# Attention in plain float32 on four 64x64 quarters of the array

## The chip, the cores and the metric

The kernel runs on one core of a Trainium2 chip. The time is the device time of one execution in microseconds. Before the change it is 1518.6 us, the median of three runs (1517.89 to 1519.48). A core has engines that run beside each other, each with its own list of instructions in order: PE (TensorE, matrix products; its weight loads are shown as PEld), DVE (VectorE), ACT (ScalarE), POOL (GpSimd) and SP, whose list issues most DMAs.

## What is computed

The reference, cut to what matters (q, k and v are 8 x 8 x 576 x 64; x has 4608 tokens of 512):

```
chunk = 64                                    # each head attends within chunks of 64 tokens
scores = (q_c @ k_c.T) / sqrt(64)
attn = exp(scores - max(scores)); attn = attn / (sum(attn) + 1e-9)
x = attn @ v_c                                # then heads side by side: 4608 x 512
h = x @ w_in;  g = softplus(h);  x = g @ w_out                # 512 -> 2048 -> 512
out = max(x @ w1, x @ w2, x @ w3) @ w_out2                    # 512 -> 768 -> 512
```

The inputs of the two layers (weights) are float64 in their stored form, so the kernel converts them first.

## The kernel before

**Tiles.** The 4608 tokens are cut into 9 blocks of 512 (TB), the 8 heads into 4 pairs (HP). A tile `t` of attention is one block and one pair of heads; there are 36, of which the first 8 (`attention_first`) come while weights are still converted and the other 28 (`attention`) while the first layer runs. A tile holds 8 chunks for each of two heads, 16 small problems of 64 x 64.

**Two ways of multiplying.** The large products (`mlp1`, lines 748 and 768) cut each float32 operand into a rounded high part and the rest, a low part, and add three fast products (high x high, high x low, low x high: `PASS`). The later tiles do so too: `do_s` (L672) makes the scores of a tile from 4 x 3 matmuls, `do_v` (L725) the second products (softmax times v) from 8 x 3. As a matmul contracts over 128 partitions and a problem has 64, one operand is laid out as blocks with zeros beside them (`fill`, into slots that POOL sets to zero in `zeros`, L1101). The first eight tiles use plain float32 matmuls, with zeros too (`big["f", t]`, set by DVE at L508): turns of q and k through a product with the identity (`turn_in`, L531), scores (L562), a turn of the softmax (`turn`, L522) and second products (L611). The later tiles turn q and k with DVE's transpose of 32 x 32 blocks (L638, L643) and the softmax with such a transpose (L700) and a trip through DRAM (`pd`, L704 and L708).

**From scores to x.** The softmax (L484 to L489) works on an SBUF copy of the scores; `to_x` copies the second products from PSUM as high part and subtracts for the low part, in two halves, since the result of `do_v` stands on 64 partitions.

**What sets the order.** All work is a list of operations with costs per engine, due times and buffers. A planner (`Plan.order`) goes through it in simulated time: when an engine is idle it takes the ready operation with the earliest due time whose buffers are free. What comes out is the fixed order of every engine. PSUM has the buffers `ph` (two of one bank), `acc` (two of two banks, the sums of a block) and `aps` (one of two banks), which the later tiles use for scores and products. Tile `t` has its scores due two steps and its products 0 steps ahead of `due_v`; a step is one slice of 128 hidden columns of the first layer. DMAs of q, k, v and of the trip through DRAM are issued from SP's list.

Names: `s` are general slots in SBUF (weights, x, operands), `tmp` smaller ones, `g` the softplus output, `mx` the maxima and sums. L254, L256 and L261 are the lines of the helpers `copy_op` (ACT, DVE) and `tt_op` (DVE), so many operations share them.

Of the kernel before, what the change touches and what calls it, by code (L numbers as in the profile page):

```python
# [20 lines left out]
P = 128  # L21
# [157 lines left out]
def tile_kernel(ctx: ExitStack, tc: tile.TileContext, q, k, v, w_in, w_out, w1, w2, w3, wo2, out):  # L179
# [173 lines left out]
    def flat(z):  # L353
        return z.t if z.place[0] == "ph" else z.t[:, 0]
# [67 lines left out]
    def load_v(t, dst):  # L422
# [30 lines left out]
    big = {}  # L453
    last_p = []
    last_s = []
    last_t = []

    def to_x(t, pv):
        b, i = divmod(t, HP)
        x = xbuf[b, i] = slot("x")  # L460
        o4 = lambda e: pv.t.rearrange("p u (c e s) -> p (u c) e s", e=2, s=CH)[:CH, :, e, :]
        to = lambda l, r: x.t[r, l].rearrange("p (c s) -> p c s", s=CH)
# [18 lines left out]

    def softmax(pbuf, p3, wide, axis):
        mx, sm = Buf("mx"), Buf("mx")
        op({"D": 0.69}, lambda e: nc.vector.reduce_max(mx.t, p3(1), axis=axis), r=[pbuf], w=[mx], alloc=[mx, sm])  # L484
        tt_op(lambda: p3(0), lambda: p3(0), lambda: wide(mx), ALU.subtract, [mx], [pbuf])
        op({"A": 0.62}, lambda e: nc.scalar.activation(pbuf.t, pbuf.t, AF.Softplus, bias=drop[:, :1], scale=SCALE), w=[pbuf])
        op({"D": 0.69}, lambda e: nc.vector.reduce_sum(sm.t, p3(1), axis=axis), r=[pbuf], w=[sm])
        op({"D": 0.1}, lambda e: nc.vector.tensor_scalar(sm.t, sm.t, 1e-9 * float(np.exp(-DROP)), None, ALU.add), w=[sm])
        op({"D": 0.12}, lambda e: nc.vector.reciprocal(sm.t, sm.t), w=[sm])  # L489
        tt_op(lambda: p3(0), lambda: p3(0), lambda: wide(sm), ALU.mult, [sm], [pbuf])  # L490
# [3 lines left out]

# [673 lines left out]
```

## Time and profile before

| | |
|---|---|
| median of three runs | 1518.6 us (1517.89 to 1519.48) |
| the profiled execution, its own time | 1518.99 us |
| its span, first to last instruction | 1517.2 us, mean granted clock 0.999 |
| PE, PEld, DVE, ACT, POOL busy | 1497.5, 1314.8, 967.7, 592.1, 4.6 us |
| DMA | 147.29 MB, mean 97 GB/s |

An instruction's busy time reaches to its result, and results of PE come out while the next instruction already runs, so lengths of neighbouring rows overlap; the distance of two starts is what a piece of work holds the engine. A chain goes back from the last instruction to whatever released it, step by step. Idle time of an engine that nobody waits for costs nothing.

### The profile page before, as it was taken

What the parts mean: (1) busy time and instruction counts of PE and PEld (TensorE: products, weight loads), DVE (VectorE), ACT (ScalarE), POOL (GpSimd) and SP (SyncE); (2) the same over time, 40 slices, a digit from 0 to 9 for tenths busy, and PEclk for the clock granted to TensorE, in tenths of its full rate; (3) what the DMA queues carried; (4) which work ended last, traced back from release to release, by engine and by line L of the source; (5) the groups of instructions that cost most, each with busy time, mean ns of one, the idle gap of its engine ahead of it and who ended that gap; (6) DMA issues with size and microseconds to landing.
All of it is one profiled execution on the core that took longest, in us unless ns stands there. A gap on an engine that the chain in (4) does not pass through costs nothing.

```text
span 1517.2 us, 23062 instructions
## 1 busy us (share of the span) xinstructions
PE 1497.5 (99%) x8930; PEld 1314.8 (87%) x8930; DVE 967.7 (64%) x1841; ACT 592.1 (39%) x1123; POOL 4.6 (0%) x11
## 2 busy tenths in 40 slices
PE   6999999999999999999999999999999999999998
PEld 5787888888888888888888888999999999999997
DVE  7988877866776767767776465554544535445443
ACT  5754344444444344444343344432322323223221
POOL 0000000000000000000000000000000000000000
PEclk9999999999999999999999999999999999999999
DMA  8354134543434325244242231222322222222222
GB/s 266 109 153 124 58 91 103 148 108 84 133 90 108 98 56 146 70 105 102 73 122 80 70 98 49 77 72 83 112 73 81 84 78 104 84 84 75 79 70 84
DMA packets 235214, 147.29 MB, mean 97 GB/s; under 512 B 167008, under 2 KB 202848, under 8 KB 235104
## 3 DMA queue, kind: packets, MB, share of 16 engines
q1 hardware_dynamic: 231904, 144.24, 32.9%
q10 hardware_dynamic: 3200, 1.57, 0.4%
q8 instruction: 70, 1.15, 0.3%
q14 instruction: 40, 0.33, 0.1%
HBM read 109.58 MB, written 36.18 MB: 96 GB/s over the span
## 4 chain that ended last, share of the span: by engine, by line
PE 97%; DVE 2%; DMA 1%; ACT 0%; issue 0%; ACTq 0%
PE acc L768 26%; PE ph L748 26%; PE ph L918 15%; PE one L918 12%; PE acc L1036 10%; PE aps L725 3%; PE aps L672 3%; PE acc L562 1%; DMA s<-in_q_dram 1%; PE acc L611 1%; PE ph L374 1%; PE acc L531 0%; ACT s L254 0%; DVE s L261 0%; DVE tmp L261 0%; DMA s<-wo2d 0%
## 5 line engine op out<-in xcount | busy, mean ns | idle before, releaser
L748 PE MATMUL ph<-s,s 128*128 128x512 f32 x1728 | 416.5, 390 | 1.2 <-DVE s L261 0.9
L768 PE MATMUL acc<-g,s 128*128 128x512 f32 x1728 | 415.3, 390 | 0.0
L768 PEld LDWEIGHTS acc<-g,s 128*128 128x128 f32 x1728 | 322.8, 188 | 67.2 <-issue 1.0
L748 PEld LDWEIGHTS ph<-s,s 128*128 128x128 f32 x1728 | 321.5, 188 | 67.8 <-DVE s L261 1.2
L918 PE MATMUL ph<-s,s 128*128 128x256 f32 x1944 | 267.8, 283 | 0.0
L261 DVE TENSOR_TENSOR tmp<-one,tmp 128x256 f32<-128x256 f32 x241 | 101.8, 422 | 247.0 <-PE one L918 213.2
L918 PEld LDWEIGHTS ph<-s,s 128*128 128x128 f32 x1944 | 251.8, 192 | 4.1
L254 ACT COPY tmp<-ph 128x256 f32<-128x256 f32 x268 | 100.0, 373 | 347.7 <-PE ph L918 346.5
L261 DVE TENSOR_TENSOR g<-tmp,g 128x512 fp32r<-128x512 f32 x198 | 136.1, 688 | 147.0 <-ACT g L254 146.1
L758 ACT ACTIVATE tmp<-ph 128x512 f32<-128x512 f32 x144 | 86.2, 598 | 306.5 <-PE ph L748 303.4
L918 PE MATMUL one<-s,s 128*128 128x256 f32 x1458 | 201.6, 283 | 0.0
L918 PEld LDWEIGHTS one<-s,s 128*128 128x128 f32 x1458 | 186.7, 192 | 0.2
L261 DVE TENSOR_TENSOR s<-tmp,s 64x512 fp32r<-64x512 f32 (+1 forms) x212 | 142.2, 674 | 25.0 <-ACT s L254 21.1
L1036 PE MATMUL acc<-s,g 128*128 128x512 f32 x648 | 157.0, 391 | 0.5 <-DMA s<-wo2d 0.5
L254 ACT CAST s<-tmp 128x512 fp32r<-128x512 f32 (+2 forms) x190 | 115.2, 610 | 60.1 <-DVE tmp L643 26.6
L1036 PEld LDWEIGHTS acc<-s,g 128*128 128x128 f32 x648 | 118.3, 188 | 23.3 <-DMA s<-wo2d 0.9
L254 ACT CAST g<-tmp 128x512 fp32r<-128x512 f32 x192 | 119.3, 622 | 25.6 <-PE acc L768 16.4
L261 DVE TENSOR_TENSOR tmp<-tmp,tmp 128x256 f32<-128x256 f32 (+1 forms) x152 | 83.0, 546 | 3.9
L254 ACT COPY p<-aps 64x512 f32<-64x512 f32 x50 | 29.1, 583 | 66.9 <-PE aps L672 66.5
L254 ACT COPY tmp<-acc 128x512 f32<-128x512 f32 (+1 forms) x66 | 37.3, 588 | 33.0 <-PE acc L1036 15.8
L725 PEld LDWEIGHTS aps<-s,s 128*64 128x64 f32 x672 | 44.5, 135 | 3.6
L672 PEld LDWEIGHTS aps<-s,s 128*128 128x128 f32 x336 | 44.0, 191 | 2.2
(97 smaller groups left out, 948.8 us busy)
## 6 DMA issues: line engine op xcount, KB each, us to landing
s<-wo2d SPq DMA_DIRECT2D x54, 512.0 KB, 3.3
s<-in_moe_w_out_dram SPq DMA_DIRECT2D x22, 512.0 KB, 4.6
x2d<-tmp SPq DMA_DIRECT2D x36, 256.0 KB, 2.8
s<-in_moe_w_dram SPq DMA_DIRECT2D x18, 512.0 KB, 4.1
s<-x2d SPq DMA_DIRECT2D x18, 512.0 KB, 4.6
s<-in_moe_w_in_dram SPq DMA_DIRECT2D x16, 512.0 KB, 4.8
out_dram<-tmp SPq DMA_DIRECT2D x29, 256.0 KB, 4.5
pd<-tmp SPq DMA_DIRECT2D x28, 256.0 KB, 2.1
```

The lines of the kernel that those rows point to most:

```text
L254: nc.scalar.copy(dst(), src())
L261: return op({"D": 0.69 * n}, lambda e: nc.vector.tensor_tensor(dst(), a(), b(), f), r=r, w=w, **kw)
L374: nc.tensor.matmul(o, ident, a.t, start=False, stop=False)
L562: nc.tensor.matmul(o[:, h], qT()[:, h * P:(h + 1) * P], blk[0]()[:, 2 * h:2 * h + 2].rearrange("p u e s -> p (u e s)"), start=True, stop=True,
L611: nc.tensor.matmul(o[:CH, c], rv()[:, c * CH:(c + 1) * CH], blk[1]()[:, c].rearrange("p e s -> p (e s)"), start=True, stop=True,)
L672: nc.tensor.matmul(o[:, h], Qh.t[:, l, h * P:(h + 1) * P], kb[m].t[:, 2 * h * P:2 * (h + 1) * P], start=(n == 0), stop=(n == 2),)
L725: nc.tensor.matmul(o[:CH, c], Vh.t[:, l, c * CH:(c + 1) * CH], z[m][:, c % 2, c // 4, c // 2 % 2], start=(n == 0), stop=(n == 2),)
L748: nc.tensor.matmul(ph.t, w[:, wi, kk * P:(kk + 1) * P], x[kk].t[:, xi], start=(kk == 0 and wi == 0 and xi == 0), stop=(kk == KD - 1 and wi ...
L758: in_line("y", op({"A": 0.6}, lambda e: nc.scalar.activation(l.t, ph.t, AF.Softplus), r=[ph], w=[l], alloc=[l]))
L768: nc.tensor.matmul(acc[m // 2].t[:, m % 2], w[:, wi, m * P:(m + 1) * P], g.t[:, gi, :], start=(first and wi == 0 and gi == 0), stop=(last ...
L918: nc.tensor.matmul(dst(), ws.t[:, wi, col + kk * P:col + (kk + 1) * P], x.t[:, xi, kk * HT:(kk + 1) * HT], start=(first and kk == 0 and wi ...
L1036: nc.tensor.matmul(acc[t // 2].t[:, t % 2], g.t[:, gi, t * P:(t + 1) * P], wo.t[:, wi], start=(j == 0 and wi == 0 and gi == 0), stop=(j == ...
```

## The change

Every product of attention becomes a plain float32 matmul of 64 x 64 by 64 columns, `square(dst, w, x, r, k)`: it contracts over the half `r` of the partitions and writes the half `k` of the output's partitions, in the bank `r`. The loop `four` goes through the pairs (r, k) in the order (0,0), (1,0), (0,1), (1,1). Operands stand without zeros, two problems on the two halves of the partitions. High and low parts of q, k, v and the softmax, the zeroed slots and `fill` are gone; only x is still cut in two, in one piece of 128 partitions. The softmax reads the scores in PSUM. For the later tiles, scores of tile `t` and the second products of tile `t - 1` are one operation (`products`) on one PSUM buffer `G`, so there is a call more at the end. v is loaded by halves of the partitions. `early` may use the slots that the zeroed blocks held.

The diff, cut to its core:

```diff
+    def load_v(t, dst, parity):
         for o, n, b, s in pieces(t):
-            for h in range(2):
-                def fn(dma, o=o, n=n, b=b, s=s, h=h):
-                    dma(
-                        out=dst().rearrange("p (c d) -> p c d", d=CH)[h * CH:(h + 1) * CH, o // CH:(o + n) // CH, :],
-                        in_=v[b, t % HP * 2 + h, s:s + n, :].rearrange("(c s) d -> s c d", s=CH),
-                    )
-                yield fn
+            c, m, first = o // CH, (o + n) // CH, s // CH
+            for half in range(2):
+                if parity:
+                    mine = [i for i in range(c, m) if i % 2 == half]
+                else:
+                    mine = [i for i in range(c, m) if i // HP == half]
+                if not mine:
+                    continue
+                at, step = first + mine[0] - c, 1 + parity
+                lo = mine[0] // 2 if parity else mine[0] % HP
+                for h in range(2):
+                    def fn(dma, half=half, mine=len(mine), at=at, step=step, lo=lo, h=h, b=b):
+                        dma(
+                            out=dst().rearrange("p (c e d) -> p c e d", e=2, d=D)[half * CH:(half + 1) * CH, lo:lo + mine, h, :],
+                            in_=v[b, t % HP * 2 + h].rearrange("(c s) d -> s c d", s=CH)[:, at:at + (mine - 1) * step + 1:step, :],
...
+    four = [(0, 0), (1, 0), (0, 1), (1, 1)]
+    def square(dst, w, x, r, k):
+        nc.tensor.matmul(dst[ROWS[k], r], w[ROWS[r]], x[ROWS[r]], start=True, stop=True)
...
-        for e, r in enumerate(ROWS):
-            copy_op(
-                lambda r=r: to(0, r),
-                lambda e=e: o4(e),
-                [pv],
-                [(x, ("h", e))],
-                psum=True,
-                alloc=[x] if e == 0 else [],
-            )
-        for e, r in enumerate(ROWS):
-            tt_op(
-                lambda r=r: to(1, r),
-                lambda e=e: o4(e),
-                lambda r=r: to(0, r).bitcast(F32),
-                ALU.subtract,
-                [pv, (x, ("h", e))],
-                [(x, ("l", e))],
-            )
-    def softmax(pbuf, p3, wide, axis):
+        to = lambda l: view(x.t[:, l], True)
+        copy_op(lambda: to(0), lambda: view(pv.t, False), [(pv, "v")], [(x, "h")], psum=True, alloc=[x])
+        tt_op(
+            lambda: to(1),
+            lambda: view(pv.t, False),
+            lambda: to(0).bitcast(F32),
+            ALU.subtract,
+            [(pv, "v"), (x, "h")],
+            [(x, "l")],
...
+        op({"D": 0.69}, lambda e: nc.vector.reduce_max(m4(), s4(), axis=AX.X), r=[(sc, "s")], w=[mx], alloc=[mx, sm])
+        tt_op(
+            p4, s4, lambda: m4()[:, :, :, None].to_broadcast([P, 2, HP, CH]), ALU.subtract, [(sc, "s"), mx], [pbuf], alloc=[pbuf]
+        )
...
+    def scores(dst, qT, kT):
+        for c in range(HP):
+            for e, h in four:
+                at = slice((h * HP + c) * CH, (h * HP + c + 1) * CH)
+                square(dst.t[:, :, c * CH:(c + 1) * CH], qT()[:, at], kT()[:, at], e, h)
...
+        def turn(e):
+            for n, src in enumerate((rq, rk)):
+                i = src().rearrange("p (e g d) -> p e g d", e=2, d=D)
+                for g in range(HP):
+                    for r, k in four:
+                        at = n * (TB // 2) + g * CH
+                        square(pq.t[:, :, at:at + CH], i[:, k, g], ident[:, r * CH:(r + 1) * CH], r, k)
+        op({"P": 1.4}, turn, r=reads(bq, "q") + reads(bq, "k"), w=[pq], alloc=[pq])
...
-        def do_s(e):
-            o = sc.t.rearrange("p u (h f) -> p (u h) f", h=2)
-            for h in range(HP):
-                nc.tensor.matmul(
-                    o[:, h],
-                    qT()[:, h * P:(h + 1) * P],
-                    blk[0]()[:, 2 * h:2 * h + 2].rearrange("p u e s -> p (u e s)"),
-                    start=True,
-                    stop=True,
-                )
-        o = op(
-            {"P": 1.9},
-            do_s,
-            r=[(bT, ("qT", 0)), (bT, ("qT", 1)), (s1[0], 0), (s1[0], 1)],
-            w=[sc],
-            alloc=[sc],
-            due=due_s,
-        )
+        o = op({"P": 0.9}, lambda e: scores(sc, qT, kT), r=[(bv, "qT"), (bc, "kT")], w=[(sc, "s")], alloc=[sc], due=due_s)
...
+        pp = Buf(*two_ps)
+        def turn_p(e):
+            for c in range(2):
+                for f in range(2):
+                    for r, k in four:
+                        at, u = (c * 2 + f) * CH, f * HP + c * 2 + k
+                        square(pp.t[:, :, at:at + CH], pbuf.t[:, u * CH:(u + 1) * CH], ident[:, r * CH:(r + 1) * CH], r, k)
+        o = op({"P": 0.9}, turn_p, r=[pbuf], w=[pp], alloc=[pp], due=due_p)
...
+            v4 = rv().rearrange("p (c e d) -> p c e d", e=2, d=D)
+            p4 = pT().rearrange("p (c e s) -> p c e s", e=2, s=CH)
+            for c in range(HP):
+                for r, k in four:
+                    square(pv.t[:, :, c * CH:(c + 1) * CH], v4[:, c, k], p4[:, c, k], r, k)
+        op({"P": 0.9}, do_v, r=reads(bv, "v") + [(bc, "pT")], w=[(pv, "v")], alloc=[pv], due=due_v)
...
+        G = Buf("aps")
+        old = before.pop() if before else None
+        def products(e):
+            if old:
+                v4 = old[1].t.rearrange("p (c e d) -> p c e d", e=2, d=D)
+                p4 = old[2].t.rearrange("p (a u i) -> p u a i", a=2, i=32)
+                for c in range(HP):
+                    for r, k in four:
+                        at = slice(TB // 2 + c * CH, TB // 2 + (c + 1) * CH)
+                        square(G.t[:, :, at], v4[:, c, k], p4[:, k * HP + c], r, k)
+            if t < NTILE:
+                scores(G, lambda: qT.t, lambda: kT.t)
+        parts = [(G, "v")] * (old is not None) + [(G, "s")] * (t < NTILE)
...
-        fill(kb, kT, 32)
-        sc = Buf("aps")
-        def do_s(e):
-            o = sc.t.rearrange("p u (h f) -> p (u h) f", h=2)
-            for h in range(HP):
-                for n, (l, m) in enumerate(PASS):
-                    nc.tensor.matmul(
-                        o[:, h],
-                        Qh.t[:, l, h * P:(h + 1) * P],
-                        kb[m].t[:, 2 * h * P:2 * (h + 1) * P],
-                        start=(n == 0),
-                        stop=(n == 2),
-                    )
...
+            {"P": 0.5 * len(parts) + 0.4},
+            products,
+            r=(list(old[1:]) if old else []) + ([qT, kT] if t < NTILE else []),
+            w=parts,
+            alloc=[G],
+            after=last_t[-1:],
+            due=T0 + STEP * (4 * (t - 1 - HP) + 2.25),
...
+            to_x(old[0], G, view)
+        if t == NTILE:
+            return
         pbuf = Buf("p")
-        for c, r in enumerate(ROWS):
-            copy_op(
-                lambda r=r: pbuf.t[r].rearrange("p (a h i) -> p h a i", a=4, h=HP),
-                lambda r=r, c=c: sc.t.rearrange("p u (h c a i) -> p (u h) c a i", c=2, a=4, i=32)[r, :, c],
-                [sc],
-                [(pbuf, c)],
-                psum=True,
-                alloc=[pbuf] if c == 0 else [],
-            )
-        softmax(
-            pbuf,
-            lambda red: pbuf.t.rearrange("p (b u i) -> p u b i" if red else "p (b u i) -> p b u i", b=2, i=32),
-            lambda z: z.t[:, None, :, None].to_broadcast([P, 2, H, 32]),
-            AX.XY,
-        )
+        softmax(G, pbuf)
...
-        fill(pb, pT, CH)
-        pv = Buf("aps")
-        def do_v(e):
-            o = pv.t.rearrange("p u (c f) -> p (u c) f", f=P)
-            z = [l.t.rearrange("p (c g h e k j) -> p c h k e g j", c=2, g=2, h=2, e=2, k=2) for l in pb]
-            for c in range(NC):
-                for n, (l, m) in enumerate(PASS):
-                    nc.tensor.matmul(
-                        o[:CH, c],
-                        Vh.t[:, l, c * CH:(c + 1) * CH],
-                        z[m][:, c % 2, c // 4, c // 2 % 2],
-                        start=(n == 0),
-                        stop=(n == 2),
-                    )
...
+        before.append((t, Rv, pT))
...
-            a, t, _ = conv(wo2, ("out", n), ("x",), after=after)
-            z = slot("x")
+            a, t, _ = conv(wo2, ("out", n), ("z", "x"), after=after)
+            z = slot("z", "x")
...
-    def zeros(name, after):
-        big[name] = [slot("z", shape=[P, 2 * TB]) for _ in range(2)]
-        for z in big[name]:
-            op({"G": 0.9}, lambda e, z=z: nc.gpsimd.memset(z.t.bitcast(F32), 0.0), w=[(z, "z")], alloc=[z], after=after)
...
+            if t <= NTILE:
```

How it moves instructions, at three places.

PE in the middle of the first layer, before: two groups of large products, the scores of one tile (`s_95`, `s_99` are the laid-out k, `s_105` q), and the next large product. The second products of the same tile's neighbour come as a group of their own later.

```order
L768 MATMUL acc_93<-g_73,s_101_1684 128x512 x6
L768 MATMUL acc_92<-g_73,s_101_1684 128x512 x6
L672 MATMUL aps_91<-s_95_1534,s_105_1834 128x256
L672 MATMUL aps_91<-s_99_1634,s_105_1834 128x256
L672 MATMUL aps_91<-s_95_1534,s_105_1834 128x256 x2
...
L672 MATMUL aps_91<-s_95_1534,s_105_1834 128x256
L748 MATMUL ph_90<-s_53_778,s_78_1192 128x512 x3
```

The same place now (line 685 is the old 768, 665 the old 748): second products of a tile (`tmp_75` the turned softmax, `rv_85` v) and scores of the next (`tmp_79` k, `tmp_77` q).

```order
L685 MATMUL acc_93<-g_72,s_87_1849 128x512 x6
L685 MATMUL acc_92<-g_72,s_87_1849 128x512 x6
L471 MATMUL aps_91<-tmp_75,rv_85 64x64 x16
L471 MATMUL aps_91<-tmp_79,tmp_77 64x64 x16
L685 MATMUL acc_93<-g_73,s_91_1946 128x512 x6
```

12 matmuls here and 24 elsewhere became 16 and 16 smaller ones that stand together, with nothing between them.

PE at the start, before: q and k of a tile are turned in two groups with a PSUM buffer each.

```order
L531 MATMUL acc_92<-ident,s_2_182 64x128 x8
L531 MATMUL acc_93<-ident,s_2_182 64x128 x8
L531 MATMUL aps_91<-ident,s_4_184 64x128 x8
L531 MATMUL acc_92<-ident,s_4_184 64x128 x8
L562 MATMUL acc_93<-s_1_180,s_3_183 128x256 x4
```

And now: one group turns both, and the scores of the first tile (`s_15`, `s_2`) are a group of 16.

```order
L471 MATMUL acc_92<-ident,s_1_180 64x64 x32
L471 MATMUL acc_93<-ident,s_3_182 64x64 x32
L471 MATMUL acc_92<-s_15_267,s_2_181 64x64 x16
L471 MATMUL acc_93<-ident,s_5_184 64x64 x32
L471 MATMUL aps_91<-s_20_327,s_4_183 64x64 x16
```

The four groups of 8 for two tiles became two groups of 32.

DVE at the start, before: slots set to zero, then the convert of the first weights, copies of turned q and k, and the first maximum from an SBUF copy (`tmp_77`).

```order
L508 MEMSET s_1_180 128x1024
L508 MEMSET s_11_198 128x1024
...
L331 SCALAR_TENSOR_TENSOR s_25_273<-s_10_190,tmp_76 128x512
L256 COPY s_5_185<-aps_91 64x512
L256 COPY s_11_198<-acc_92 64x8x64
L484 TENSOR_REDUCE mx_67<-tmp_77 128x8
L261 TENSOR_TENSOR tmp_77<-tmp_77,mx_67 128x512
```

And now: the convert comes first, copies are of full height, and the maximum is taken from PSUM (`acc_92`).

```order
L331 SCALAR_TENSOR_TENSOR s_13_262<-s_9_188,tmp_76 128x512
L256 COPY s_15_267<-acc_92 128x512
L256 COPY s_20_327<-acc_93 128x512
L493 TENSOR_REDUCE mx_67<-acc_92 128x8
L261 TENSOR_TENSOR tmp_77<-acc_92,mx_67 128x512
```

The eight memsets are gone, and the copy of the scores ahead of the maximum with them.

## Rows read from the trace of the kernel before

**Rows 1.** The page: busy time of the engines, and the chain by engine.
```profile
PE 1497.5 (99%) x8930; PEld 1314.8 (87%) x8930; DVE 967.7 (64%) x1841; ACT 592.1 (39%) x1123; POOL 4.6 (0%) x11
...
PE 97%; DVE 2%; DMA 1%; ACT 0%; issue 0%; ACTq 0%
```
**Rows 2.** PE's longest waits: waiting line, releaser, total us, times, longest.
```profile
PE acc L531 <- DMA s<-in_q_dram: 5.5, 1, 5.5
PE acc L611 <- ACT s L254: 2.5, 1, 2.5
PE acc L531 <- ACT s L254: 2.2, 1, 2.2
```
**Rows 3.** The chain at the start: start us, length us, engine, line.
```profile
11.87 1.92 PE acc L531 x8
...
45.36 0.69 DVE s L261
...
46.09 1.06 PE acc L531 x8
...
54.04 2.75 PE ph L748 x12
```
**Rows 4.** Stretches: busy us (instructions) of each engine, PEclk, DMA share, GB/s.
```profile
11.00:46.10 35.10, 28.20 (x161) 21.84 (x161) 29.47 (x63) 24.64 (x44) 0.00 (x0) 0.95 0.85 257
...
300.00:500.00 200.00, 200.00 (x1067) 168.88 (x1066) 144.07 (x256) 85.69 (x145) 0.00 (x0) 1.00 0.40 104
500.00:700.00 200.00, 200.00 (x1067) 168.89 (x1066) 142.76 (x252) 80.82 (x137) 0.00 (x0) 1.00 0.38 96
```
**Rows 5.** PE's groups by form: operands, records, busy us, mean ns, idle before.
```profile
L725 PE MATMUL aps<-s,s 128*64 128x128 f32 x672 | 44.9, 223 | 0.0
L672 PE MATMUL aps<-s,s 128*128 128x256 f32 x336 | 44.7, 283 | 0.0
...
L562 PE MATMUL acc<-s,s 128*128 128x256 f32 x48 | 12.2, 402 | 0.3 <-ACT s L254 0.3
...
L562 PE MATMUL aps<-s,s 128*128 128x256 f32 x16 | 3.9, 386 | 0.2 <-ACT s L254 0.2
```
**Rows 6.** PE's timeline at 509 to 519 us: start us, length us.
```profile
509.86 1.60 PE L725 MATMUL aps<-s,s 128*64 128x128 f32 x24
511.31 2.96 PE L748 MATMUL ph<-s,s 128*128 128x512 f32 x12
...
516.82 1.60 PE L672 MATMUL aps<-s,s 128*128 128x256 f32 x12
518.26 2.00 PE L748 MATMUL ph<-s,s 128*128 128x512 f32 x8
```
**Rows 7.** PE's timeline at 77 to 88 us.
```profile
77.78 1.96 PE L611 MATMUL acc<-s,s 128*64 128x128 f32 x16
79.67 0.66 PE L522 MATMUL acc<-ident,tmp 128*128 128x128 f32 x4
...
83.46 3.71 PE L611 MATMUL acc<-s,s 128*64 128x128 f32 x32
87.10 0.50 PE L373 MATMUL ph<-s,s 128*128 128x512 f32 x1
```
**Rows 8.** PE in 46.1 to 95 us: lines L531, L562, L522, L611 alone, in turn.
```profile
46.10:95.00 48.90, 7.11 (x56) 1.00 0.28 87
46.10:95.00 48.90, 7.66 (x32) 1.00 0.28 87
46.10:95.00 48.90, 2.52 (x16) 1.00 0.28 87
46.10:95.00 48.90, 9.59 (x80) 1.00 0.28 87
```
**Rows 9.** DVE's groups in 0 to 60 us.
```profile
L508 DVE MEMSET s<- 128x1024 f32 x8 | 7.3, 912 | 2.1 <-issue 1.1 <-PEq L1150 1.0
...
L261 DVE TENSOR_TENSOR s<-acc,s 64x512 fp32r<-64x512 f32 x6 | 4.1, 684 | 0.3 <-ACT s L254 0.2
...
L261 DVE TENSOR_TENSOR s<-aps,s 64x512 fp32r<-64x512 f32 x2 | 1.4, 684 | 0.0
```
**Rows 10.** L725's matmuls: duration ns min/median/max, first and last start us.
```profile
L725 PE MATMUL aps<-s,s x672: 221/222/225, 215.1 to 857.6; 128*64 128x128 f32 x168
```
**Rows 11.** DVE's and ACT's groups: part of the softmax, and its transpose.
```profile
L486 ACT ACTIVATE p<-p,drop 128x512 f32<-128x512 f32 x28 | 20.2, 722 | 3.8 <-DVE p L261 3.7
...
L700 DVE STREAM_TRANSPOSE tmp<-p 128x512 f32<-128x512 f32 x28 | 19.8, 706 | 0.5
```
**Rows 12.** DMA issues: count, KB each, median us from issue to landing.
```profile
pd<-tmp SPq DMA_DIRECT2D x28, 256.0 KB, 2.1
tmp<-pd SPq DMA_DIRECT2D x112, 64.0 KB, 2.0
```
**Rows 13.** PE's weight loads at 509 to 512 us.
```profile
509.64 1.68 PEld L725 LDWEIGHTS aps<-s,s 128*64 128x64 f32 x24
```
**Rows 14.** PE's weight loads by form, columns as in rows 5.
```profile
L748 PEld LDWEIGHTS ph<-s,s 128*128 128x128 f32 x1728 | 321.5, 188 | 67.8 <-DVE s L261 1.2 <-ACT s L254 1.0 <-issue 0.5
...
L725 PEld LDWEIGHTS aps<-s,s 128*64 128x64 f32 x672 | 44.5, 135 | 3.6
```

More of the change, by code (lines that the diff above doesn't have):

```diff
@@ L506, in attention_first @@
         due_s, due_p = due_v - 12.0, due_v - 4.0
-        for z in s1 if t < HP else ():
-            op({"D": 0.6}, lambda e, z=z: nc.vector.memset(z.t, 0.0), w=[(z, "z")], alloc=[z])
-        blk = [lambda z=z: z.t.rearrange("p (u e s) -> p u e s", e=2, s=CH) for z in s1]
         engs = "SA" if t < HP else "S"
         first = -60.0 + 4.0 * t if t < HP else None
-        loads(load_plain(t, q, rq), bq, "q", 1.1, allocs[0], engs, after, first)
-        loads(load_plain(t, k, rk), bk, "k", 1.1, allocs[1], engs, after, first)
@@ L514, in attention_first @@
-        loads(load_v(t, rv), bv, "v", 1.6, allocs[2], engs, after, first and first + 10.0)
-        pq, pk = Buf(*two_ps), Buf(*two_ps)
-        def turn(dst, src):
-            def fn(e):
-                o = flat(dst)
-                for h in range(HP):
-                    nc.tensor.transpose(o[:, h * P:(h + 1) * P], src(h), ident)
-            return fn
-        def turn_in(dst, src):
-            def fn(e):
-                i = src().rearrange("p (h g d) -> p h g d", h=2, d=D)
-                for h in range(2):
-                    for g in range(HP):
-                        nc.tensor.transpose(dst.t[:D, h, g * P:(g + 1) * P], i[:, h, g, :], ident)
-            return fn
@@ L535, in in_order @@
-        def in_order(z, e):
-            return z.t[:D, e].rearrange("p (g c m) -> p c m g", g=HP, c=NC)
-        op({"P": 1.0}, turn_in(pk, rk), r=reads(bk, "k"), w=[pk], alloc=[pk])
-        for e, r in enumerate(ROWS):
+        loads(load_plain(t, q, rq), bq, "q", 1.1, [bq], engs, after, first)
+        loads(load_plain(t, k, rk), bq, "k", 1.1, (), engs, after, first)
+        loads(load_v(t, rv, 1), bv, "v", 1.6, [bv], engs, after, first and first + 10.0)
+        pq = Buf(*two_ps)
+        def turn(e):
[5 more added lines that the diff above has]
+                        square(pq.t[:, :, at:at + CH], i[:, k, g], ident[:, r * CH:(r + 1) * CH], r, k)
@@ L595, in attention_first @@
[L595 to L605 removed]
+        softmax(sc, pbuf)
@@ new lines, in attention_first, with attention, view @@
+        to_x(t, pv, view)
+    before = []
+    def attention(t, after=()):
+        if t < NTILE:
+            Rq, Rk, Rv = Buf("rq"), Buf("rk"), Buf("rv")
+            qT, kT = Buf("tmp"), Buf("tmp")
+            loads(load_32(t, q, lambda: Rq.t), Rq, "q", 2.2, [Rq], after=after)
+            loads(load_32(t, k, lambda: Rk.t), Rk, "k", 2.2, [Rk], after=after)
+            loads(load_v(t, lambda: Rv.t, 0), Rv, "v", 1.6, [Rv], after=after)
+            op({"D": 0.69}, lambda e: nc.vector.transpose(qT.t, Rq.t), r=[Rq], w=[qT], alloc=[qT])
+            op({"D": 0.69}, lambda e: nc.vector.transpose(kT.t, Rk.t), r=[Rk], w=[kT], alloc=[kT])
+        G = Buf("aps")
[8 more added lines that the diff above has]
+                        square(G.t[:, :, at], v4[:, c, k], p4[:, k * HP + c], r, k)
+            if t < NTILE:
+                scores(G, lambda: qT.t, lambda: kT.t)
+        parts = [(G, "v")] * (old is not None) + [(G, "s")] * (t < NTILE)
+        op(
+            {"P": 0.5 * len(parts) + 0.4},
[5 more added lines that the diff above has]
+            due=T0 + STEP * (4 * (t - 1 - HP) + 2.25),
+        )
+        if old:
+            def view(z, flat):
+                if flat:
+                    return z.rearrange("p (r f) -> p r f", r=2)
+                return z[:, :, TB // 2:]
+            to_x(old[0], G, view)
+        if t == NTILE:
+            return
+        pbuf = Buf("p")
+        softmax(G, pbuf)
```

166 lines of the change are left out of this document (41 added, 125 removed).

## The prediction

> **What bounds the kernel now.** I read the page's head first, then the waits of TensorE, then its groups by form, then single stretches. The page gives PE 99% of the span and 97% of the chain that ended last [rows 1]; the reader should check at once whether that is one long queue of work or many small waits. It is a queue: the longest three waits of PE come to 5.5, 2.5 and 2.2 us, each once, and no attention line of the long middle stretch (L672, L725) is among them [rows 2]. DVE is at 64%, ACT at 39% [rows 1]. So a microsecond of PE work taken away after the start is a microsecond of time, and work taken from DVE or ACT there is worth nothing by itself.
>
> Two stages have to be kept apart. Until about 46 us the chain runs over data that lands, then over DVE (0.69 us pieces up to 45.36); from 46.09 us on it is PE without a break, and the first matmul of the large products comes at 54.04 us [rows 3]. Between 11 and 46.1 us PE is busy 28.2 of 35.1 us and DVE 29.5 [rows 4].
>
> **What the 28 later tiles cost on PE now.** The busy column overstates it, since the last result of a group is still in flight while the next group starts: L672 and L725 are 44.7 and 44.9 us busy [rows 5], 1.60 us for each group, but the next line's first matmul starts 1.45 us after L725's and 1.44 us after L672's [rows 6]. I use the starts: 2.89 us per tile, 24 records at 60 ns and 12 at 120 ns.
>
> **What they would cost afterwards.** Scores and second products of a tile are 16 matmuls each of 64x64 by 64 columns in float32. In the trace a float32 matmul leaves two records: L562 has 4 matmuls per tile over 8 tiles and 48 + 16 records [rows 5]. So a tile has 64 records of 64 columns. The price of such a record is not in the trace; the nearest is L611, plain float32 with 64 weight columns and 128 moving ones. Its group of 16 takes 1.89 us from start to next start, its group of 32 takes 3.64 [rows 7]; the difference gives 109 ns a record and leaves 0.14 us that a group costs once. Half the columns make 55 ns, an estimate that assumes the time goes with the columns; L725 against L672 shows that (60 ns for 128 columns, 120 for 256).
>
> The 0.14 us I read as the price of going into and out of the array's divided form: L611 has outputs on 64 partitions, its neighbours on 128. The Trainium skill (TensorEngine Tiling (Array Packing), Tiling Modes, Key Properties) says that a change of tiling mode, unlike a change of tile, drains the engine. That rule speaks against a change that enters and leaves the mode 29 times; it gives no figure, and the trace agrees as far as 0.14 us can show it. Quarters cut rows as well as columns, which no row here shows, so I take twice that, 0.28 us per group, with 0 and 0.4 as bounds.
>
> The open question is how many of the four quarters work at once. The ends:
> - all four: 64 x 55/4 ns = 0.88 us, with the group's price 1.16 us; saved 1.73 us per tile, 48.4 us in 28 tiles;
> - one at a time: 64 x 55 ns = 3.52 us, with the price 3.80 us; lost 0.91 us per tile, 25.5 us in all.
> The break-even is (2.89 - 0.28)/64 = 41 ns per record, between the two. No row shows two quarters at work. I take all four: the four matmuls of a round go to four different pairs of contraction half and output half, the halves write different banks, the 16 stand in one row of the order with nothing between them, and the columns are what the rows above are priced by. [...]
>
> **The first eight tiles.** Each has four PE groups after the change: turning q and k (32 matmuls), scores, turning the softmax, products (16 each), 160 records. What lies after 46.1 us counts in full: L531, L562, L522 and L611 are 7.1 + 7.7 + 2.5 + 9.6 = 26.9 us busy there, with 56, 32, 16 and 80 records [rows 8]. Taking some 0.15 us of overlap off each of the 16 groups leaves 24.5 us. That is 3.5 tiles' turns, 4 scores, 4 turns of the softmax and 5 products, so afterwards 3.5 x 64 + 13 x 32 = 640 records: at 13.75 ns 8.8 us, with 17 groups x 0.28 us 13.6 us; saved 10.9 us. One at a time it would be 35.2 + 4.8 = 40.0 us, lost 15.5.
>
> Before 46.1 us PE is not what ends last, so I count DVE there. Gone are 8 memsets (7.3 us [rows 9]), but they run while the first data are still on their way (PE's first work is at 11.87 us [rows 3]), so they hide behind the load; of the 8 half-height subtractions for the first four x tiles (5.5 us [rows 9]) four full-height ones remain, 2.8 us less; some copies from PSUM go, mostly ACT's. I take 4 us, between 0 (the convert of the weights fills DVE again) and 9.
>
> **What else moves.** Per later tile the high/low splits of q, k, v and the softmax go, some 16 DVE and ACT instructions, all beside PE; 4 POOL memsets go, off the path. Loads of v become four DMAs for each piece instead of two on SP's queue; the DMA engines are 38% to 40% busy in the middle stretch [rows 4], so I cost them at nothing. If that cover were gone, the next q and k would be late, and the new group is where it would be felt.
>
> The new wait: products of a tile and scores of the next stand in one PE row after another and share one PSUM buffer, so a late q, k or softmax stops everything queued behind on PE. From the scores to the products there is one tile's distance. L725 starts from 215.1 to 857.6 us for 28 tiles [rows 10], 23.8 us apart. In between lie seven instructions of DVE and ACT, of about 0.7 us each where they are full-size [rows 11], some 5 us, then two DMA hops of 2.1 and 2.0 us [rows 12] and five issues: about 11 us. It must be over 12 us late before PE waits, and today PE never waits for L725. I cost it at nothing.
>
> **The sum.** From the profiled execution's own 1519.0 us (span 1517.2; the median of the three timed runs, 1518.6, is the same within 0.4): 1519.0 - 48.4 - 10.9 - 4 = 1455.7, so 1456 us. Best bounds of every term (no group price, 9 us at the start): 28 x 2.01 + 15.7 + 9 = 81 us less, 1438.
>
> **Rivals.**
> - *Pairs.* The two records of one matmul fall on the same quarter one after the other. If products start strictly in order, the second waits for the first's stream and holds up the next quarter; only its own stream runs beside the next matmul. Then it is 55 ns per matmul, 27.5 per record: 64 x 27.5 ns + 0.28 = 2.04 us, saved 0.85 us per tile, 23.8 us; at the start 24.5 - 22.4 = 2.1, and 4; 1489 us. For it: both records need the same part of the array, and the order puts no other matmul between them. Against it: no row says that a quarter that is busy holds up the next one. The Trainium skill (TensorE: Matmul & The Clock Gate, Part 3, The mechanism) calls matmuls strictly first in, first out in start and end; by that rule this rival is what follows.
> - *One at a time, slower.* If weight loads take turns, the quarters bring nothing: a tile has 64 loads of 64 columns, and L725's 24 loads of 64 columns take 1.68 us from the first's start to the last's end, 67 ns apart [rows 13]. It decides from 41 ns per record on. Priced at 55 ns: 1519.0 + 25.5 + 15.5 - 4 = 1556 us. For it: in no row do loads come closer than about one per product. Against it: there they never had to. The Trainium skill (the same page, Part 2, LDWEIGHTS) sets a load at its columns over 1.2 GHz, 53 ns for 64; the trace agrees in size (135 against 188 ns for 64 and 128 columns [rows 14], 53 ns for the 64 between), but whether loads of different quarters overlap no run here shows.
> - *The group waits.* If the softmax's round trip or q and k come late by more than the 12 us, each microsecond costs 28. Half a microsecond per tile would give back 14 us: 1470. The chance is small by the margin above.
>
> **Chances.** All four quarters, up to 1470 us: 0.55; pairs or something between: 0.27; one at a time: 0.12; waits: 0.06. Faster by over 0.2% (3 us, about what a measurement can tell from no change) holds the first two and most of the last, 0.85; the same 0.03; slower 0.12. The range runs from 1438 to 1500: pairs with 10 us of new waits still lie in it, one at a time does not. The likeliest case's own range is 1438 to 1470.
>
> **What would show it.** The records of the new matmul line: about 14 ns apart means four, 28 pairs, 55 one at a time; a group of two parts ending some 1.2, 2.0 or 3.8 us after it began, by the start of the next line. The gap on either side of a group shows the 0.28. PE's idle time must stay near 20 us; a wait at the new line on DVE, or on the small DMAs, would be the third rival. The first large product should come at about 45 to 50 us instead of 54. The forecast is wrong if the group takes over 1.6 us, or if PE's busy share falls below 98%.

## The result and the profile after

The changed kernel takes 1499.5 us (median of 4 runs, 1495.99 to 1503.33) against 1519.0 us, a ratio of 0.987 (95% interval 0.985 to 0.990). It is faster, but the gain is 19.5 us where 63 were forecast. That the time lies in the forecast's range is luck: the range's upper end was made of pairs with 10 us of new waits, and no pairs were found. The profiled execution took 1499.52 us, with a span of 1497.7.

The page after: busy time, granted clock in 40 slices, chain by engine (against [rows 1]).

```profile
PE 1445.6 (97%) x10642; PEld 1250.0 (83%) x10642; DVE 790.6 (53%) x1562; ACT 456.5 (30%) x890; POOL 0.7 (0%) x7
...
PEclk7999999999998999999999999999999999999999
...
PE 93%; DMA 2%; DVE 1%; SPq 1%; ACT 1%; issue 1%; ACTq 0%; DVEq 0%
```

PE is at 97%, so 52 us of the span are idle by this count, where before it was 20. The prediction named a share under 98% as a sign that it is wrong. The clock dips at the start and in a slice of the middle, around 470 us. The next view is PE's waits (waiting line, releaser, total us, times, longest), against [rows 2].

```profile
PE acc L685 <- ACT tmp L254: 14.4, 5, 4.7
PE acc L471 <- DVE s L256: 6.6, 1, 6.6
PE aps L471 <- DMA tmp<-pd: 6.1, 3, 5.1
```

L685 is the second product of the first layer, L471 every attention matmul. The first and third waits are new, and both sit in the long middle stretch, where PE had no wait over 1 us before; the second is new too, at the start. The attention groups themselves do what the forecast said: PE's timeline where a group stands (start us, length us):

```profile
362.26 0.69 PE L471 MATMUL aps<-tmp,rv 64*64 64x64 f32 x32
362.78 0.65 PE L471 MATMUL aps<-tmp,tmp 64*64 64x64 f32 x32
```

64 records start within 0.94 us, 15 ns each, against 14 forecast for four quarters at once. So the arithmetic got cheap, and the time went elsewhere. PE's total between 40 and 800 us says how much; one row of the stretch view for each kernel, before first and after second (PE busy is the first number behind the 20th of a second's 760 us, then PEld, DVE, ACT, POOL, granted clock, DMA share, GB/s).

```profile
40.00:800.00 760.00, 757.93 (x3976) 633.58 (x3975) 573.94 (x1046) 336.50 (x570) 3.82 (x4) 1.00 0.40 104
```

```profile
40.00:800.00 760.00, 732.12 (x5321) 591.87 (x5320) 424.66 (x808) 223.03 (x377) 0.00 (x0) 0.98 0.41 107
```

Idle time went from 2.1 to 27.9 us, and the clock from 1.00 to 0.98. One of the places, in the timeline of all engines (the bracket is the idle time before a row and what ended it):

```profile
458.14 0.59 ACT L254 COPY tmp<-acc 128x512 f32<-128x512 f32 x1 [0.81 <-DVE g L261]
458.32 5.40 PEld L665 LDWEIGHTS ph<-s,s 128*128 128x128 f32 x24
458.54 5.60 PE L665 MATMUL ph<-s,s 128*128 128x512 f32 x24
460.24 0.38 SPq L719 DMA_DIRECT2D x2d<-tmp  x1
460.66 0.43 SPq L289 DMA_DIRECT2D s<-in_moe_w_dram  x1
463.65 0.59 ACT L254 COPY tmp<-acc 128x512 f32<-128x512 f32 x1 [4.92 <-DMA x2d<-tmp]
464.26 0.33 SPq L719 DMA_DIRECT2D x2d<-tmp  x1
466.65 1.74 SPq L642 DMA_DIRECT2D tmp<-pd  x4
469.19 0.28 PEld L471 LDWEIGHTS aps<-tmp,rv 64*64 64x64 f32 x2 [5.48 <-issue]
469.22 0.44 PE L471 MATMUL aps<-tmp,rv 64*64 64x64 f32 x2 [5.08 <-DMA tmp<-pd]
...
471.98 5.08 PE L685 MATMUL acc<-g,s 128*128 128x512 f32 x12
...
472.19 0.69 DVE L256 COPY tmp<-acc 128x512 f32<-128x512 f32 x1 [14.14 <-PE aps L471]
...
476.89 2.91 PE L665 MATMUL ph<-s,s 128*128 128x512 f32 x12
```

A block of the first layer has just ended, and its sums must be copied from `acc` into `tmp` buffers. ACT's first copy finds one; its second waits 4.92 us for a store to `x2d` to land (the one issued at 460.24), which frees a buffer; the softmax's way back from DRAM (`tmp<-pd`) needs a `tmp` too and is issued only at 466.65; PE stands for 5.08 us. Then the clock: the group of 12 large products at 471.98 takes 5.08 us where a group of the same shape and number takes 2.91 at 476.89. The stretches tell the same (columns as above):

```profile
440.00:460.00 20.00, 19.70 (x146) 16.07 (x146) 11.71 (x22) 7.79 (x13) 0.00 (x0) 1.00 0.38 91
460.00:470.00 10.00, 4.58 (x21) 3.38 (x19) 0.00 (x0) 0.59 (x1) 0.00 (x0) 0.81 0.44 135
470.00:480.00 10.00, 9.94 (x88) 8.25 (x89) 6.68 (x13) 3.81 (x7) 0.00 (x0) 0.68 0.27 80
480.00:500.00 20.00, 20.00 (x148) 16.39 (x147) 7.25 (x14) 4.71 (x8) 0.00 (x0) 1.00 0.40 93
```

The trace has 1.2 GHz, the lower level, from 466.2 us on for 10.2 us. After 100 us there are four more such stretches: 3.4 us at 196.5, 3.4 at 370.6, 3.4 at 575.4 and 6.8 at 671.0; each of the last three begins within a long wait of PE (3.4 to 4.7 us) or about 1 us after it, that at 196.5 behind one of 2.0 us.

Why is no `tmp` free? There are nine. The transposes of q and k (L594, L595) put their results there. The view of one line (count, duration ns min/median/max, first and last start us) has for the q transposes, and for the scores that read them:

```profile
L594 DVE STREAM_TRANSPOSE tmp<-rq x28: 670/711/716, 103.0 to 729.7; 128x512 f32<-128x512 f32 x28
...
L471 PE MATMUL aps<-tmp,tmp x896: 218/218/311, 151.0 to 812.7; 64*64 64x64 f32 x180
```

The last q stands turned 83 us before it is used. Counted tile by tile, from tile 16 to 32 four tiles' q have been turned when a group starts, its own among them, and nearly always their k too: eight of the nine buffers. In the kernel before, the same two views are

```profile
L638 DVE STREAM_TRANSPOSE tmp<-rq x28: 702/704/712, 114.4 to 814.1; 128x512 f32<-128x512 f32 x28
...
L672 PE MATMUL aps<-s,s x336: 277/283/283, 187.7 to 832.8; 128*128 128x256 f32 x168
```

and the last q stands 19 us ahead. There they could not run ahead: k's transpose (L643) waited for the softmax transpose of the tile before (`after=last_p[-1:]`), and q's (L638) took the single slot `Qh` with it (`alloc=[qT, Qh]`). Both conditions are gone in the diff, the slot with the high and low parts of q that it held.

### The profile page after: what moved, and what is told of

It reads as the page before. It is cut to its first block, busy times and chain, and to the rows that moved or that the text cites. A ratio compares the mean times of both kernels' runs of the same rounds, so it can differ in the third digit from the quotient of the medians.

```text
span 1497.7 us, 26084 instructions
## 1 busy us (share of the span) xinstructions
PE 1445.6 (97%) x10642; PEld 1250.0 (83%) x10642; DVE 790.6 (53%) x1562; ACT 456.5 (30%) x890; POOL 0.7 (0%) x7
## 4 chain that ended last, share of the span: by engine, by line
PE 93%; DMA 2%; DVE 1%; SPq 1%; ACT 1%; issue 1%; ACTq 0%; DVEq 0%
PE acc L685 26%; PE ph L665 25%; PE ph L835 16%; PE one L835 12%; PE acc L953 10%; PE aps L471 2%; PE acc L471 1%; DMA x2d<-tmp 1%; PE ph L374 1%; DMA s<-in_q_dram 1%; SPq L438 1%; SPq L413 1%; ACT s L254 0%; PE ph L373 0%; ACT tmp L675 0%
## 5 line engine op out<-in xcount | busy, mean ns | idle before, releaser
L685 PE MATMUL acc<-g,s 128*128 128x512 f32 x1728 | 426.6, 396 | 18.4 <-ACT tmp L254 14.4
L685 PEld LDWEIGHTS acc<-g,s 128*128 128x128 f32 x1728 | 326.1, 190 | 90.3 <-ACT tmp L254 15.9
L303 DVE TENSOR_SCALAR tmp<-s 128x512 int32<-128x512 int32 x56 | 23.5, 420 | 116.3 <-PE aps L471 107.0
L254 ACT CAST s<-tmp 128x512 fp32r<-128x512 f32 (+1 forms) x103 | 61.7, 604 | 27.9 <-DVE tmp L322 14.1
L254 ACT COPY tmp<-acc 128x512 f32<-128x512 f32 x48 | 27.7, 588 | 85.8 <-PE aps L471 27.2
L261 DVE TENSOR_TENSOR s<-tmp,s 128x512 fp32r<-128x512 f32 (+1 forms) x72 | 46.3, 654 | 7.5 <-ACT s L254 6.7
L256 DVE COPY tmp<-acc 128x512 f32<-128x512 f32 x17 | 11.8, 692 | 59.9 <-ACT tmp L254 39.8
L322 DVE SCALAR_TENSOR_TENSOR tmp<-s,tmp 128x512 int32<-128x512 int32 x56 | 38.3, 683 | 0.4
```

What stands on the lines that cost most here:

```text
L254: nc.scalar.copy(dst(), src())
L261: return op({"D": 0.69 * n}, lambda e: nc.vector.tensor_tensor(dst(), a(), b(), f), r=r, w=w, **kw)
L303: lambda e: nc.vector.tensor_scalar(ai(), hw(), 0x7FFFFFFF, None, ALU.bitwise_and),
L322: lambda e: nc.vector.scalar_tensor_tensor(ai(), hw(), -0x40000000, ai(), ALU.bitwise_and, ALU.bitwise_or),
L685: nc.tensor.matmul(acc[m // 2].t[:, m % 2], w[:, wi, m * P:(m + 1) * P], g.t[:, gi, :], start=(first and wi == 0 and gi == 0), stop=(last ...
```

## Experiments

The theory after the result: q and k that run ahead fill `tmp`, and the waits and the half clock behind them cost some 35 us. Rivals: the v loads, which now hold SP's queue; the joint group of products and scores, which makes one wait for the other; too few buffers as such. A ratio, with its 95% interval, is to the kernel before, run on the same chip.

**q and k in other buffers.** `qk_slot`:

```diff
-            qT, kT = Buf("tmp"), Buf("tmp")
+            qk = slot("qh", "vh", dt=F32)
```

> Theory (small buffers): the later tiles' turned q and k now wait in two of the nine tmp buffers until the shared group, so at a block's end the four copies of the sums out of PSUM find no free tmp buffer until a store lands, and the large products wait for the PSUM sums. Here q and k sit in the slots qh and vh, idle in this stretch. Expected: PE's waits on the ACT copies (14.4 us) and on the small DMAs (6.1 us) go, the half clock after 100 us goes with them (27 us of it in the changed kernel), 1499.5 falls by 30 to 42 us, to 1458 to 1470. Rival (v's loads block SP's list while they wait for the one buffer of v): the waits stay, 1495 to 1500. Rival (the shared group itself comes too late): the waits stay, 1495 to 1500.

Measured: 1465.4 us, 0.965 (0.964 to 0.967). The waits for `tmp` are gone, and no stretch at half clock stands between 200 us and the last 3 us of the span. 34 us of the missing gain were there.

**A second v buffer.** `rv2`:

```diff
-            Rq, Rk, Rv = Buf("rq"), Buf("rk"), Buf("rv")
+            Rq, Rk = Buf("rq"), Buf("rk")
+            Rv = Buf("rv", "vh", ...)
```

> A second buffer for v of the later tiles, in slot vh, nothing else. Rival (v's loads stand in SP's list ahead of the stores of the sums and wait for the group to free the one buffer): the loads are issued early, the stores behind them too, PE's 14.4 us of waiting on the ACT copies mostly goes, 1499.5 falls to 1465 to 1480. Theory (small buffers): the copies still lack tmp buffers, 1495 to 1503. Rival (the group itself late): 1495 to 1503.

Measured: 1498.1 us, 0.987 (0.985 to 0.989). PE's waits stay as they were (L691 is L685 of after):

```profile
PE acc L691 <- ACT tmp L254: 14.1, 5, 4.6
...
PE aps L471 <- DMA tmp<-pd: 6.0, 3, 4.9
```

The rival of the v loads falls.

**Scores and products apart.** `apart` gives the second products a group of their own:

```diff
-        before.append((t, Rv, pT))
+        W = Buf("aps")
...
+        op({"P": 0.9}, second, r=[Rv, pT], w=[(W, "v")], alloc=[W], due=T0 + STEP * (4 * (t - HP) + 2.25))
```

> Undoes one part: scores and second products of a tile are two groups again, each in its own PSUM buffer, as before; all else as in the changed kernel. Rival (sharing the group holds everything up): the waits after 100 us go (34 us with the half clock), a second entry into and out of the divided form costs 28 x 0.35 = 10 us, 1470 to 1480. Theory (small buffers): q and k are held for a shorter time, so part of the waits go, but the copies still compete with them; the second group costs its 10 us: 1485 to 1502.

Measured: 1503.1 us, 0.990 (0.988 to 0.991). That is 1 us above the theory's range and far from the rival's. Waits of 13.7 us for `tmp` remain, now at the activation's output (`PE ph <- ACT tmp`), so sharing a group isn't what stalls. `apart_qk` is the same edit on `qk_slot`, where nothing else waits:

> The run qk_slot with scores and second products in two groups. With the waits gone in both, the difference is the price of entering and leaving the divided form once more per tile. By the changed kernel's rows that is 92 ns at the entry, 148 less 15 ns after the last record and 112 ns on the next matmul, 0.34 us: 28 x 0.34 = 9.5 us, so 1465.4 + 9.5 = 1475 (1472 to 1478). If sharing the group has a price of its own in waits, less than 1470; if nothing is paid twice, 1465.

Measured: 1472.5 us, 0.970 (0.968 to 0.971), 7.1 us more than `qk_slot`, 0.25 us for each of the 28 groups more. By the starts of the records, two groups hold PE 0.36 us longer than a shared one, some 10 us in all. Most of the difference is a wait of 1.9 us at 192.3 us and 3.4 us of half clock from 195.3 us, which only `qk_slot` has. So sharing saves 0.25 to 0.36 us per tile.

**Same quarter in a row.** `same_quarter` puts the four matmuls of a quarter one after another:

```diff
-        for c in range(HP):
-            for e, h in four:
+        for e, h in four:
+            for c in range(HP):
```

> The 16 matmuls of the later tiles' scores and of their products in another order: the four of one quarter of the array after each other, then the next quarter. If quarters work side by side only because consecutive matmuls go to different ones, a record takes some 55 ns instead of 15 and a shared group 3.5 to 3.8 us instead of 1.1: 28 x 2.5 = 70 us more, some 1570. If a quarter can queue several products while others start, or the order doesn't matter, the group stays at 1.1 us and the time at 1495 to 1503.

Measured: one run, 1533.3 us. PE's timeline of a group (start us, length us):

```profile
374.73 1.36 PE L471 MATMUL aps<-tmp,rv 64*64 64x64 f32 x29
...
376.11 1.31 PE L471 MATMUL aps<-tmp,tmp 64*64 64x64 f32 x29
378.27 1.66 PE L685 MATMUL acc<-g,s 128*128 128x512 f32 x6 [0.85 <-DVE tmp L256]
```

The 64 records now take 2.47 us from the first to the last start, 39 ns each instead of 15. They start 58 ns apart where one quarter works alone; at each change of quarter some start only 4 to 6 ns behind another, which I read as the next quarter's. That is why it isn't 58 throughout, and why the time lies between the two that were expected. From a group's first start to the next line's, 2.62 us pass instead of 1.09. So the gain does come from quarters at work at once, and the order of the loop decides how many.

**The lost wait alone.** `guard` puts a wait on the softmax transpose of the tile before on both transposes, and changes nothing else (that transpose is noted in `last_p`; for q the wait stands in for the slot `Qh`):

```diff
-            op({"D": 0.69}, ... qT.t, Rq.t), r=[Rq], w=[qT], alloc=[qT])
-            op({"D": 0.69}, ... kT.t, Rk.t), r=[Rk], w=[kT], alloc=[kT])
+            op({"D": 0.69}, ... alloc=[qT], after=last_p[-1:])
+            op({"D": 0.69}, ... alloc=[kT], after=last_p[-1:])
```

> No buffer is added. The kernel before let DVE turn a tile's k only after the transpose of the previous tile's softmax, and q only into one slot; the change took both away, and in its trace the turned q and k of up to four tiles lie in eight of the nine tmp buffers, some 90 us ahead of their group. Here both turns wait again for the transpose of the previous softmax. Theory (run-ahead): at most one tile ahead, the copies of the sums find buffers, PE's 20 us of waits after 100 us and the half clock go: 1460 to 1472. Rival (nine tmp buffers are too few for the shared group whatever the order, and the two slots helped as room): the waits stay at least in half, 1480 to 1500.

Measured: 1464.4 us, 0.964 (0.962 to 0.965), as good as other buffers. The same views as above, line, then stretch:

```profile
L594 DVE STREAM_TRANSPOSE tmp<-rq x28: 669/688/711, 102.5 to 762.6; 128x512 f32<-128x512 f32 x28
...
L471 PE MATMUL aps<-tmp,tmp x896: 218/218/267, 150.5 to 777.9; 64*64 64x64 f32 x180
```

```profile
40.00:800.00 760.00, 755.77 (x5532) 613.46 (x5530) 438.19 (x828) 233.91 (x392) 0.00 (x0) 1.00 0.42 110
```

The last q is 15 us ahead instead of 83, PE is idle for 4.2 us instead of 27.9, the clock is at 1.00. The span is 34.7 us shorter: 23.7 us of idle time, and the rest at most half of the 23.8 us of half clock after 300 us, 11.9, which makes 35.6 (PE stands still in a part of them).

**Fewer buffers.** `qk_tmp7` is `qk_slot` with seven `tmp` (`mem("tmp", 9, ...)` becomes 7).

> q and k in the slots qh and vh as in the run qk_slot, which took 1465.4 us, but seven tmp buffers instead of nine, so the room is that of the changed kernel. Theory (run-ahead: two slots let at most two tiles wait and keep them out of tmp): up to 5 us of new waits at the most, 1464 to 1472. Rival (room): the waits at the block ends come back, 1485 to 1500.

Measured: 1464.7 us, 0.964 (0.963 to 0.966). The text above is wrong in one point: a slot holds both q and k of a tile, so the two slots are worth four `tmp`, and the room is 11 buffers, not 9. What the run shows is that seven `tmp` are enough for everything but q and k. That nine are enough for all is shown by `guard`: the nine were not too few, they were taken too early. That the buffers do the harm, and not the early loads themselves, is supported by this run and `qk_slot`, where q still stands turned some 45 us ahead, outside `tmp`, and nothing waits; no run let four tiles run ahead outside `tmp`.

**The start.** The first large product comes at 51.3 us, where 45 to 50 were forecast and 53.8 was measured before (the chain has it at 54.04 [rows 3]). ACT's first rows in after, and in `guard_vsp` (below):

```profile
0.77 1.54 ACTq L399 DMA_DIRECT2D s<-in_q_dram  x3
2.34 3.34 ACTq L438 DMA_DIRECT2D s<-in_v_dram  x2
6.97 0.38 ACTq L399 DMA_DIRECT2D s<-in_q_dram  x1
8.38 5.84 ACTq L438 DMA_DIRECT2D s<-in_v_dram  x6
14.26 0.59 ACT L254 COPY s<-acc 128x512 f32<-128x512 f32 x1 [12.25 <-DMA s<-in_v_dram]
```

```profile
0.76 2.59 ACTq L399 DMA_DIRECT2D s<-in_q_dram  x4
5.14 0.38 ACTq L399 DMA_DIRECT2D s<-in_k_dram  x1
7.62 0.59 ACT L254 COPY s<-acc 128x512 f32<-128x512 f32 x1 [5.61 <-PE acc L471]
```

ACT issues eight v pieces ahead of its first copy, and the last six hold it until 14.2 us. In `guard_vsp` PE's wait of 6.6 us for DVE's copy (the second of the waits above) is down to 0.7 us. `qk_vsp` is `qk_slot` with these loads on SP alone, `guard_vsp` is `guard` with the same edit:

```diff
-        loads(load_v(t, rv, 1), bv, "v", 1.6, [bv], engs, after, first and first + 10.0)
+        loads(load_v(t, rv, 1), bv, "v", 1.6, [bv], "S", after, first and first + 10.0)
```

> The run qk_slot with v of the first tiles loaded from SP's list alone instead of SP's and ACT's. In the changed kernel ACT's list issues twice as many v loads before its first copy, and that copy starts at 14.28 us instead of 11.24. If those loads hold ACT up, the first copy comes at 11 to 12.5 us and the end 1.5 to 3 us earlier: 1462.5 to 1464. Rival (the q and k data themselves land later, or later links of the start absorb it): 1465 to 1467.

Measured: 1463.3 us, 0.963 (0.962 to 0.965), 2.2 us under `qk_slot`, within the two intervals.

> The changed kernel with two edits: the transposes of a later tile's q and k wait for the softmax transpose of the tile before (as in the kernel with that wait alone, 1464.4 us), and the second half of the first tiles' v loads is issued by SyncE alone. With the slots for q and k the second edit brought ScalarE's first copy from 14.26 to 7.55 us and took 4.8 us of TensorE's idle time at the start, and the time fell by 2.2 us only, since a stretch at half clock became longer. Theory (the clock takes most of an earlier start back): 1460 to 1464 us, 0.962 of the time before. Rival (the start counts in full): 1457 to 1460 us.

Measured: 1460.9 us, 0.961 (0.960 to 0.963), the lowest median of the study. The span is 4.1 us under that of `guard`; the intervals touch, so this edit's own share is not settled by the times.

**Is it the clock that holds the start?** To `guard_vsp`, `busy` adds 20 groups of four matmuls whose sums nobody reads, to keep PE at work at the start; `busy_start` keeps the 10 that ran before 32 us. They follow the first four tiles, and in `busy_start` the first two; the text of `busy` says eight.

```diff
+            def fn(e, z=z):
+                for _ in range(4):
+                    nc.tensor.matmul(z.t[:, :P], ident, ident, start=True, stop=True)
```

> The same kernel with TensorE given more to do at the start: after each of the first eight tiles' scores three groups, and after each softmax turn two groups, of four float32 matmuls of 128x128 whose sums nobody reads. It tells whether the stretches at half clock at the start (13.7 us from 22 us and 6.8 us from 66 us in the run with the slots) follow the idle time of TensorE before them. Theory: they do, so the stretches shrink or go, the granted clock of the first 80 us rises above 0.9, and the time falls by up to 7 us to 1455 to 1461 us. Rival: the clock does not answer to this, or the added groups delay the real ones as much: the same stretches, and 1463 to 1470 us.

> The kernel with added matmuls at the start, with only those that ran before 32 us (10 groups of four; 80 records, 10.3 us busy there). The other ten groups ran after 60 us, 9.8 us of TensorE where every microsecond counts. In the run with all twenty no stretch at half clock was left before 66 us. Theory (the clock follows TensorE's idle time, and the loss of that run was the ten late groups): the time falls by about 9.8 us from 1467.7 to 1456 to 1460 us, under the 1460.9 without any added matmul, with the granted clock at 1.00 from 0 to 60 us. Rival (the added groups cost what the clock gives): 1461 to 1465 us.

Measured: `busy` 1467.7 us, 0.966 (0.965 to 0.967); `busy_start` 1461.6 us, 0.962 (0.961 to 0.964), the same as without. The stretches of the start, `guard_vsp` first, `busy_start` second:

```profile
0.00:20.00 20.00, 11.58 (x452) 9.60 (x452) 12.56 (x26) 8.15 (x13) 0.73 (x7) 1.00 0.64 186
20.00:40.00 20.00, 13.43 (x276) 8.46 (x277) 15.68 (x39) 7.22 (x14) 0.00 (x0) 0.66 0.83 271
40.00:60.00 20.00, 19.41 (x464) 14.35 (x454) 17.85 (x39) 13.46 (x25) 0.00 (x0) 1.00 0.45 109
60.00:80.00 20.00, 17.27 (x184) 13.38 (x183) 15.98 (x37) 6.08 (x11) 0.00 (x0) 0.91 0.60 207
```

```profile
0.00:20.00 20.00, 13.12 (x448) 11.21 (x452) 13.04 (x27) 7.65 (x12) 0.73 (x7) 1.00 0.69 201
20.00:40.00 20.00, 18.56 (x429) 15.18 (x422) 17.18 (x42) 9.31 (x17) 0.00 (x0) 1.00 0.81 260
40.00:60.00 20.00, 19.91 (x402) 14.45 (x403) 16.53 (x35) 11.81 (x21) 0.00 (x0) 1.00 0.44 114
60.00:80.00 20.00, 16.87 (x179) 13.08 (x178) 15.30 (x35) 6.82 (x12) 0.00 (x0) 0.83 0.57 195
```

With PE busy for 18.56 instead of 13.43 us from 20 to 40 us the clock stays up, 1.00 instead of 0.66: here the clock does follow PE's idle time. But the time stays. The first large product starts at 39.8 instead of 44.1 us, but the ninth activation behind such products at 109.7 instead of 109.9. What was won is waited away in between: PE waits 3.1 us for DVE's `tmp` in front of an attention group, and 6.8 us of half clock from 63.3 us follow. So my theory for the clock held and the one for the time fell: what PE gains there it loses in waits for DVE. What would shorten DVE's part was not tried.

## What of the prediction was right, and the step that failed

- **Four quarters at once: right.** 15 ns a record against 13.75 by the estimate; before, a tile took 2.89 us of PE by its starts [rows 6]. The rival *Pairs* has fallen: behind the first round records start four within 20 ns, and the next four 58 ns later. As records of one quarter stand 58 ns apart (`same_quarter`), I take these four to belong to four quarters. The strict order that the Trainium skill states (TensorE: Matmul & The Clock Gate, Part 3, The mechanism) does not make one matmul's second record hold up the other quarters here.
- **The group's price: right in size.** I took 0.28 us for going in and out of the divided form. The record starts leave 0.09 us more than usual in front of a shared group, 0.05 in its first round, 0.11 behind its last and 0.11 behind the next matmul: 0.36 us, under my bound of 0.4, and 1.30 us for the whole group where 1.16 were forecast. An added group costs 0.25 us by the times (`apart_qk`). A price at each change agrees with the rule of the Trainium skill (TensorEngine Tiling (Array Packing), Tiling Modes) that a change of mode drains the engine.
- **The 28 later tiles: nearly right, once nothing waits.** By the starts a shared group adds 1.30 us to PE's row in `guard`, with what it delays on either side; the two groups before add 2.95 in the same count. That is 1.65 us saved per tile, 46 us in all, against 1.73 and 48.4. The times bear it out: from the ninth activation of the first layer on (119.0 us before, 112.5 with `guard`) to the end of the span, before takes 1398.2 us and `guard` 1350.5, 47.7 us less. But `guard` has by then done 72 of the 1728 matmuls of the first layer's second product (L685) and before 51 (L768); 21 of them, 0.227 us apart, are 4.8 us of work. Without them the tiles bring 43 us. `guard` also has a wait of 1.9 us at 193.7 and 3.4 us of half clock from 196.2, which take up most of the rest.
- **The start: too high by some 4 us.** I had 10.9 + 4 = 14.9 us. Up to the same activation, with those 4.8 us counted for it, it was 10.8 in after, 11.3 in `guard` and 13.9 in `guard_vsp`. Where I let the v loads cost nothing, ACT's eight of them held its first copy; and 20.5 us at half clock stand before 54 us in after where before had 3.4.
- **"What else moves", with "I cost it at nothing": the step that failed.** The margin of 12 us was that of the softmax's round trip, and it was right for that: in `guard`, PE waits at most 0.8 us in all at the later tiles' groups. I priced the buffers of the changed kernel nowhere: "What else moves" let the splits of q and k go for free, and with them went the slot and the wait that kept q and k one tile ahead. They ran up to three tiles ahead of the next group, held with its own eight of nine `tmp`, and at four block ends between 363 and 673 us the copies of the sums, or the softmax on its way back, waited for a `tmp`. That is 1499.5 - 1464.4 = 35.1 of the 44 us missing (`guard`). The third rival was the nearest, with another cause: not data too late, but data too early. Nor had I a price for the half clock behind such waits, up to a third of the loss.

With the wait put back the kernel takes 1464.4 us, 8.7 us over the sum's 1455.7; some 5 of them lie in the later tiles and 4 in the start.

## What to carry to other kernels

When a change drops an operation, list what that operation made others wait for, by its buffers and its order: a wait that costs nothing may be what keeps a shared pool free. In a plan that takes ready work early, loads with a free path run ahead until their buffers are gone, and the shortage shows elsewhere, as waits for a store to land. Price a wait of TensorE with the slow stretch behind it, and test the suspected condition alone.

## What the runs showed of the hardware

- The records of 64x64 float32 matmuls by 64 columns (two for each matmul) start every 15 ns on average when the quarter changes at each matmul; with the four matmuls of a quarter in a row, every 39 ns.
- A group of 64 such records between large products costs PE 0.36 us beyond its 64 x 14.6 ns, of which 0.11 us fall on the next large product.
- PE's waits of 3.4 to 5.1 us in the middle of the first layer went with 3.4 to 10.2 us at 1.2 GHz, which began within the wait or up to 1.1 us after it; at that level 12 large products took 5.08 us instead of 2.91. Waits of 1.9 us went either way: 3.4 us at 1.2 GHz follow in `guard` (from 196.2 us), none in `guard_vsp`. Added matmuls at the start took the stretch of 13.7 us (from 22.1 us) away, the granted clock of 20 to 40 us rising from 0.66 to 1.00.
